# Fewer fp32 steps in the second layer, and an earlier split of four weight rows

## The chip, the cores and the metric

One core of one Trainium2 chip runs the kernel. The metric is the device time of one execution in microseconds, as the median of several runs. TensorE (PE) multiplies matrices, VectorE (DVE), ScalarE (ACT) and GpSimd (POOL) work on tiles in on-chip memory, and SyncE (SP) issues most of the loads and stores. Each engine works through a list of instructions of its own in a fixed order; where an instruction needs another engine's result, it waits, and everything behind it on that engine waits too.

## The reference

The reference is an attention over a small memory, followed by a feed-forward layer with a squared ReLU. There are 8 batches, 8 heads, 576 positions, a head size of 64, 32 memory slots, a model width of 512 and a hidden width of 2048; all in fp32.

```python
a = softmax(phi, axis=seq)                       # (8, 8, 576, 32)
k_m = einsum('bhsm,bhsd->bhmd', a, k)
v_m = einsum('bhsm,bhsd->bhmd', a, v)            # 32 rows of 64 for each head
attn = softmax(q @ k_m^T / 8, axis=-1)           # (8, 8, 576, 32)
x = (attn @ v_m), heads side by side             # (4608, 512)
h = maximum(x @ w_in, 0)                         # (4608, 2048)
out = (h * h) @ w_out                            # (4608, 512)
```

## The kernel before

**The algebra.** x @ w_in is never formed from x. For each batch the kernel multiplies v_m by w_in once, which gives u (32 slots x 8 heads = 256 rows, 2048 columns), and then h = attn @ u. Matmuls in full fp32 are avoided mostly: a number is split into a rounded fp32r part ("hi") and the remainder ("lo"), and a product is taken as hi x hi + lo x hi + hi x lo, three fp32r matmuls for one fp32 matmul.

**The stages.** Batches 0 and 1 go through a fused part of 56 steps (`steps`, at line 878), in which both layers are computed; later batches go through the first layer and, from about 419 us on, through a second layer of another form, neither of which the diff touches. A fused step k takes one block f of 128 hidden units and one group of tokens (b, t): 320 tokens for t = 0, 256 for t = 1. Steps 0 to 3 are f = 0 to 3 of group (0,0), steps 4 to 7 the same rows of (0,1), steps 8 to 11 of (1,0), steps 12 to 15 of (1,1). Step k consists of `ffn1` (h at L696, six matmuls; relu on ScalarE at L704; the square at L708 on ScalarE or at L710 on VectorE), then of half-step 2k of the side work, then of `ffn2` of step k - 2 (`LEAD = 2`; the second layer, sums in the accumulators acc), then of half-step 2k + 1.

**Whole and split rows.** In a step below `WHOLE` with f in 0 to 3, the second layer is done in full fp32: g is one fp32 tile and `ffn2` has four matmuls (L739; the trace has two records for each). In other steps ScalarE writes g_hi with a second square (L720), VectorE or GpSimd writes g_lo (L724; VectorE if k is in `LO_DVE`), and `ffn2` has twelve fp32r matmuls (L747) on a split weight row. `SQ_ACT` names the steps whose square is on ScalarE.

**The weights.** They come as 64-bit words and are decoded (`decode`): ScalarE reads a tile twice (L599, L602), VectorE has three instructions (L604, L607, L612), and VectorE or GpSimd the last (L619). Rows f = 0 to 3 of w_out are decoded whole for the fp32 steps; `split_out` later splits such a row: a copy (L670) and a cast (L676) on ScalarE, a DMA of the whole row that ScalarE issues (L678), and the remainder on VectorE (L679).

**The attention of a group.** Scores on PE (L429), a transpose on VectorE (L460), the maximum (L466), the difference (L472), the exponential on ScalarE (L474), the sum (L477), the reciprocal (L483), the product (L488), the transpose back (L491), then a_hi on ScalarE (L494) and a_lo on GpSimd (L495). h of the group's first step needs both. The scores of group (1,0) need the memory of batch 1 (`task_mem`: L361, L371, L387 to L398, and copies to the tile mem at L406 by VectorE and ScalarE).

**What sets the order.** `loads` is the order in which the first tiles are asked for on SP's queue, of which eight may be under way at a time. The string `order` interleaves, by generator steps, the exponentials, memories, decodes (d0 to d3), attention (a0, a1) and u of batch 0 ahead of step 0. `plan` is a table of side work: each entry names a generator and the half-steps at which its successive pieces are issued. An earlier half-step puts a piece ahead of more work in every engine's list that it uses; it is no time.

Of the kernel before, what the change touches and what calls it, by code (L numbers as in the profile page):

```python
# [24 lines left out]
def attn_moe_kernel(ctx: ExitStack, tc: tile.TileContext, qT, kv, phi, w_in, w_out, outT):  # L25
# [659 lines left out]
    def ffn1(f, parts, T, turn, square, whole):  # L685
# [237 lines left out]
    def next_kv():  # L923
# [30 lines left out]
    later = [x[0] for x in loads].index(task_phi)  # L954
    for fn, *args in loads[:later]:
# [28 lines left out]
    for n in kept:  # L984
# [2 lines left out]


    plan = [
        ((3, 5, 5, 6, 6, 7), task_exp, 1),  # L990
        ((6, 6, 7), decode_out, 2, nc.vector, True),
        ((1,), fetch_w_in, 5, 1),
        ((14, 16, 16), decode_in, 2, 0, nc.gpsimd),
        ((13,), fetch_w_in, 6, 1),
        ((11,), fetch_w_in, 4, 0),
        ((10, 10, 10, 10, 11, 11, 12), task_attend, 1, 0),
        ((11,), fetch_w_in, 5, 0),
# [4 lines left out]
        ((21,), fetch_w_in, 7, 1),
        ((21, 22, 22), decode_in, 3, 1, nc.vector),
        ((26,), fetch_w_in, 7, 0),
        ((25, 29, 29), task_u, 1, 1),
        ((44, 44, 44), decode_in, 5, 1, nc.vector),
        ((45,), fetch_w_out, 10),
        ((31, 32, 33), decode_in, 4, 0, nc.vector),
        ((28,), fetch_w_in, 6, 0),
# [3 lines left out]
        ((25, 30, 30, 32, 32), decode_out, 5, nc.vector),
        ((32, 34, 37), task_u, 0, 1),
        ((33, 34, 35, 37, 40), decode_out, 7, nc.vector),
        ((17, 22, 22), decode_in, 3, 0, nc.vector),
        ((40, 42, 42), decode_in, 4, 1, nc.vector),
        ((50, 51, 54, 54, 54), decode_out, 10, nc.vector),
        ((46, 47, 47, 50, 51), decode_out, 8, nc.gpsimd),
        ((55,), fetch_w_out, 11),  # L1020
        ((54, 55, 55, 56, 59), decode_out, 9, nc.vector),
        ((20, 23, 24, 26, 27), decode_out, 4, nc.vector),
        ((36,), fetch_w_out, 9),
        ((49, 50, 51), task_u, 0, 2),
        ((58,), fetch_w_out, 12),
        ((65, 68, 68), decode_in, 7, 1, nc.vector),
        ((56, 60, 61), task_u, 1, 2),
        ((60, 61, 63), decode_in, 6, 0, nc.vector),
        ((68,), fetch_w_out, 15),
        ((70, 72, 73, 75, 77), decode_out, 12, nc.vector),  # L1030
        ((74,), fetch_w_out, 14),
        ((73, 73, 74), task_u, 0, 3),
        ((63, 65, 65), decode_in, 6, 1, nc.vector),
        ((58, 59, 61, 64, 65), decode_out, 11, nc.vector),
        ((66, 67, 69), decode_in, 7, 0, nc.vector),
        ((57,), task_phi, 2),
        ((76, 77, 77, 79, 79), decode_out, 13, nc.vector),
        ((53,), task_kv, 2, 0),
        ((86,), task_q, 2, 0),
        ((77, 80, 82, 83, 84, 84), task_exp, 2),  # L1040
        ((79,), task_kv, 2, 1),
        ((77, 78, 78, 79, 82), decode_out, 14, nc.vector),
# [10 lines left out]
        ((89, 90, 91, 91, 91, 94, 96), task_attend, 2, 0),
        ((91,), task_stream, 0),
        ((89,), u_slots.give, 5),
        ((89,), task_q, 2, 1),
        ((105,), task_stream, 2),
        ((97,), task_phi, 3),
        ((108,), task_q, 3, 0),
        ((90,), task_kv, 3, 0),  # L1060
        ((96,), task_kv, 3, 1),
        ((98,), task_stream, 1),
        ((101, 102, 103, 104, 105, 106, 107), task_both, 2, 1, 0),
        ((107, 108, 108, 110, 111, 113), task_exp, 3),
        ((107, 108, 109), task_u, 2, 1),
        ((2,), lambda: spin(3, ident)),
        ((2, 4, 4), decode_out, 1, nc.gpsimd, True),
        ((2,), task_q, 1, 1),
        ((2, 2, 3), task_u, 0, 0, HC, 2 * HC),
        ((8, 8, 9, 9), task_mem, 1),  # L1070
        ((5, 7, 9), decode_out, 3, nc.gpsimd, True),
        ((0, 3, 3, 4, 5, 6), lambda: start["a1"]),
# [92 lines left out]
    for k, step in enumerate(steps):  # L1165
# [346 lines left out]
```

## Time and profile before

| | |
|---|---|
| median of 3 runs | 702.66 us (701.67 to 705.85) |
| the profiled execution | 700.55 us |
| its span in the trace | 698.8 us |
| PE, VectorE, ScalarE, GpSimd busy | 98%, 74%, 58%, 9% of the span |
| granted clock of PE | 1.00 in all stages |
| moved by DMA | 133.59 MB, 191 GB/s in the mean |

The span lies 1.75 us below the time of the profiled execution. A busy share near 100% for an engine means that time can be saved only by giving that engine less to do, or by closing its few gaps; but the share is a mean over stages, so the stages are looked at one by one below. An engine's idle time costs something only where another engine waits for it.

### The profile page before, as it was taken

What the parts mean: (1) busy time and instruction counts of PE and PEld (TensorE: products, weight loads), DVE (VectorE), ACT (ScalarE), POOL (GpSimd) and SP (SyncE); (2) the same over time, 40 slices, a digit from 0 to 9 for tenths busy, and PEclk for the clock granted to TensorE, in tenths of its full rate; (3) what the DMA queues carried; (4) which work ended last, traced back from release to release, by engine and by line L of the source; (5) the groups of instructions that cost most, each with busy time, mean ns of one, the idle gap of its engine ahead of it and who ended that gap; (6) DMA issues with size and microseconds to landing.
All of it is one profiled execution on the core that took longest, in us unless ns stands there. A gap on an engine that the chain in (4) does not pass through costs nothing.

```text
span 698.8 us, 14434 instructions
## 1 busy us (share of the span) xinstructions
PE 686.7 (98%) x5860; PEld 613.1 (88%) x5860; DVE 515.2 (74%) x883; ACT 402.8 (58%) x617; POOL 59.7 (9%) x86
## 2 busy tenths in 40 slices
PE   9899999999999999999999999999999999999996
PEld 5477798978888787878787899999999999999996
DVE  4978797887756848484847305889988979697984
ACT  2647887876554454545455555575646464555551
POOL 1322102102221000000000000000000000000000
PEclk9999999999999999999999999999999999999999
DMA  9993527263694969695944468663353534434331
GB/s 309 390 330 127 205 104 236 68 212 118 195 339 169 302 229 301 208 301 191 307 177 171 161 212 298 215 196 103 111 167 105 166 107 136 136 122 151 91 121 61
DMA packets 94355, 133.59 MB, mean 191 GB/s; under 512 B 5520, under 2 KB 59408, under 8 KB 93648
## 3 DMA queue, kind: packets, MB, share of 16 engines
q1 hardware_dynamic: 91472, 127.62, 55.8%
q10 hardware_dynamic: 2816, 5.05, 2.0%
q8 instruction: 46, 0.75, 0.5%
q14 instruction: 21, 0.17, 0.1%
HBM read 86.51 MB, written 46.14 MB: 190 GB/s over the span
## 4 chain that ended last, share of the span: by engine, by line
PE 89%; DMA 5%; DVE 3%; ACT 1%; issue 0%; ACTq 0%; POOL 0%; DVEq 0%
PE b L1300 33%; PE hh L1432 22%; PE acc L747 11%; PE h L696 7%; PE ps_m L429 5%; PE b L1283 4%; PE acc L739 3%; PE h L306 2%; DMA wo<-in_w_out 1%; DMA wo<-in_w_in 1%; PE h L429 1%; DMA wo<-in_kv 1%; DMA kvb<-in_kv 1%; DVE x_lo L1234 1%; PE h L1432 0%
## 5 line engine op out<-in xcount | busy, mean ns | idle before, releaser
L1230 ACT CAST x_hi<-y 128x1792 fp32r<-128x1792 f32 (+1 forms) x56 | 88.0, 1571 | 96.5 <-PE b L1300 52.4
L1234 DVE TENSOR_TENSOR x_lo<-y,x_hi 128x1792 fp32r<-128x1792 f32 (+1 forms) x56 | 104.7, 1870 | 51.8 <-ACT x_hi L1230 49.0
L1463 ACT ACTIVATE o<-hh 128x576 f32<-128x576 f32 x94 | 61.3, 652 | 89.2 <-PE hh L1432 73.5
L1300 PE MATMUL b<-x_lo,s_hi 128*128 128x256 f32 x384 | 108.0, 281 | 0.0
L1300 PE MATMUL b<-x_hi,wo 128*128 128x256 f32 x576 | 107.9, 283 | 0.0
L1300 PE MATMUL b<-x_hi,s_hi 128*128 128x256 f32 x384 | 107.8, 281 | 0.0
L1300 PE MATMUL b<-x_hi,s_lo 128*128 128x256 f32 x384 | 107.8, 281 | 0.0
L1300 PEld LDWEIGHTS b<-x_hi,wo 128*128 128x128 f32 x576 | 89.9, 192 | 0.0
L1300 PE MATMUL b<-x_lo,wo 128*128 128x256 f32 x288 | 81.5, 283 | 0.5 <-DVE x_lo L1234 0.5
L1223 DVE TENSOR_TENSOR y<-y 128x512 f32<-128x512 f32 x144 | 73.7, 512 | 3.3
L1300 PEld LDWEIGHTS b<-x_hi,s_hi 128*128 128x128 f32 x384 | 73.7, 192 | 0.0
L1300 PEld LDWEIGHTS b<-x_lo,s_hi 128*128 128x128 f32 x384 | 72.1, 188 | 0.0
L1300 PEld LDWEIGHTS b<-x_hi,s_lo 128*128 128x128 f32 x384 | 72.1, 188 | 0.0
L1213 ACT ACTIVATE y<-raw 128x1024 f32<-128x1024 f32 (+1 forms) x56 | 57.4, 1025 | 12.1 <-DMA raw<-r_f 8.3
L1300 PEld LDWEIGHTS b<-x_lo,wo 128*128 128x128 f32 x288 | 55.3, 192 | 0.9 <-DVE x_lo L1234 0.9
L578 DVE TENSOR_TENSOR u_lo<-ps_m,u_hi 128x1024 fp32r<-128x1024 f32 (+1 forms) x33 | 38.8, 1176 | 13.3 <-ACT u_hi L576 13.1
L1432 PEld LDWEIGHTS hh<-a_hi,u_hi 128*128 128x128 f32 x188 | 29.4, 188 | 20.5 <-ACT o L1463 15.9
L1432 PE MATMUL hh<-a_hi,u_hi 128*128 128x288 f32 x188 | 43.8, 314 | 0.0
L747 PE MATMUL acc<-g_hi,wo 128*128 128x320 f32 (+1 forms) x256 | 43.2, 301 | 0.0
L1432 PE MATMUL hh<-a_hi,u_lo 128*128 128x288 f32 x188 | 40.2, 295 | 0.0
L1432 PE MATMUL hh<-a_lo,u_hi 128*128 128x288 f32 x188 | 40.1, 294 | 0.0
L704 ACT ACTIVATE r_room<-h 128x320 f32<-128x320 f32 (+2 forms) x56 | 24.7, 442 | 25.6 <-PE h L696 25.3
(240 smaller groups left out, 1435.8 us busy)
## 6 DMA issues: line engine op xcount, KB each, us to landing
r_f<-o SPq DMA_DIRECT2D x48, 576.0 KB, 3.8
raw<-r_f SPq DMA_DIRECT2D x48, 512.0 KB, 4.0
wo<-in_w_in SPq DMA_DIRECT2D x16, 512.0 KB, 8.6
wo<-in_w_out SPq DMA_DIRECT2D x16, 512.0 KB, 7.9
kvb<-in_kv SPq DMA_DIRECT2D x28, 256.0 KB, 5.2
q_sb<-in_q SPq DMA_DIRECT2D x24, 288.0 KB, 4.2
out_t<-m SPq DMA_DIRECT2D x24, 256.0 KB, 2.2
e_sb<-in_phi SPq DMA_DIRECT2D x8, 512.0 KB, 4.7
```

What stands on the lines that cost most here:

```text
L429: nc.tensor.matmul(out[half][M * pr:M * (pr + 1), :y.shape[-1]], mem[hs, x, pr], y, start=True, stop=True)
L578: nc.vector.tensor_tensor(out=u_lo[:, :, n0:n1], in0=ps[:, :, :n1 - n0], in1=u_hi[:, :, n0:n1].bitcast(F32), op=ALU.subtract)
L696: nc.tensor.matmul(h[:, at:at + n], u[:, qd, fs], x[:, qd], start=(i == 0), stop=(i == len(todo) - 1))
L747: nc.tensor.matmul(acc[e][:, :T], wo[f][:, w, e * P:(e + 1) * P], x, start=first and x is g_hi and w == 0, stop=last and x is g_lo,)
L1213: nc.scalar.activation(y[i][:, :2 * n], raw.pop(i), AF.Square)
L1223: nc.vector.tensor_tensor(out=out, in0=in0, in1=in1, op=ALU.subtract)
L1230: nc.scalar.copy(x[i][0], y[i])
L1234: nc.vector.tensor_tensor(out=x[i][1], in0=y.pop(i), in1=x[i][0].bitcast(F32), op=ALU.subtract)
L1283: nc.tensor.matmul(acc[e][:, :n], wo[f][:, v, e * P:(e + 1) * P], x[i][u][:, f % 2 * n:(f % 2 + 1) * n], start=f == 0 and j == 0, stop=f = ...
L1300: nc.tensor.matmul(acc[m][:, e * HALF:(e + 1) * HALF], w, x[i][u][:, z * HALF:(z + 1) * HALF], start=p == 0 and e == 0 and j == 0, stop=p ...
L1432: nc.tensor.matmul(banks[t][:, :T], u[:, qd, fs], x[:, qd], start=(i == 0), stop=(i == len(todo) - 1))
L1463: nc.scalar.activation(r.rearrange("p (t x) -> p t x", t=NT), h[:, :, :S // NT], AF.Relu)
```

## The change

`WHOLE` falls from 16 to 4: steps 4 to 15 take twelve fp32r matmuls in the second layer, not four in fp32, and have a g_hi and a g_lo. For that the rows f = 0 to 3 of w_out are split in half-steps 8 to 16, not 80 to 91. In steps 4 to 15, g_lo is on VectorE in steps 4, 5, 6 and 12 and on GpSimd in the others, and the square moves to VectorE in steps 7 and 13. `loads`, `order` and the places of `plan` are changed too; of `plan`'s some 85 entries the diff shows those that the text speaks of.

```diff
@@ -864,9 +864,9 @@
         yield
 
     LEAD = 2
-    SQ_ACT = (0, 1, 2, 3, 4, 5, 6, 7, 8, 9, 10, 11, 12, 13, 14, 15, 16, 17, 18, 19, 20, 21, 23, 24, 25, 26, 27, 28, 29, 30, 31, 32, 33, 34, 35, 36, 37, 39, 40, 42, 43, 44, 45, 47, 48, 50, 52, 53, 54, 55, 56, 58,)
-    LO_DVE = (-1, 16, 17, 18, 19, 20, 21, 22, 23, 27, 28, 32, 33, 34, 35, 36, 37, 39, 40, 41, 48, 49, 52, 56, 57, 58, 59, 60, 61, 62, 63, 64,)
-    WHOLE = 16
+    SQ_ACT = (0, 1, 2, 3, 4, 5, 6, 8, 9, 10, 11, 12, 14, 15, 17, 18, 20, 21, 22, 23, 25, 26, 27, 28, 29, 31, 32, 33, 34, 36, 37, 39, 40, 41, 44, 45, 46, 49, 50, 53, 54, 55, 56, 59, 60, 61,)
+    LO_DVE = (-1, 0, 1, 4, 5, 6, 12, 19, 20, 22, 23, 24, 26, 31, 36, 38, 40, 42, 43, 45, 47, 48, 49, 50, 52, 54, 56, 57, 58, 59, 62, 63, 64,)
+    WHOLE = 4
     Q4 = NFT // 4
 
 
@@ -927,29 +927,29 @@
     loads = [
         (first_phi,),
         (first_kv, 0),
+        (fetch_w_in, 0, 1),
         (first_kv, 1),
         (fetch_w_in, 0, 0),
+        (task_q, 0, 1),
         (task_q, 0, 0),
-        (task_q, 0, 1),
-        (fetch_w_in, 0, 1),
         (fetch_w_in, 1, 0),
+        (fetch_w_out, 4),
+        (fetch_w_out, 0),
         (fetch_w_in, 1, 1),
-        (fetch_w_in, 2, 0),
         (fetch_w_out, 3),
         (task_phi, 1),
+        (fetch_w_out, 5),
+        (fetch_w_out, 1),
+        (fetch_w_in, 2, 0),
+        (task_kv, 1, 0),
+        (fetch_w_out, 2),
         (fetch_w_out, 6),
-        (fetch_w_out, 0),
-        (fetch_w_out, 1),
-        (fetch_w_out, 2),
         (fetch_w_in, 3, 0),
+        (fetch_w_in, 2, 1),
         (task_q, 1, 0),
-        (fetch_w_out, 4),
+        (next_kv,),
         (fetch_w_out, 7),
-        (task_kv, 1, 0),
-        (next_kv,),
         (fetch_w_in, 3, 1),
-        (fetch_w_out, 5),
-        (fetch_w_in, 2, 1),
     ]
     later = [x[0] for x in loads].index(task_phi)
     for fn, *args in loads[:later]:
@@ -972,7 +972,7 @@
     }
 
     order = (
-        "e e e e e m d0 m m d0 d0 m d0 a0 d1 d0 d2 a1 a0 a0 a0 a0 a0 a0 d1 d1 d1 d1 d3 a0 a0 a0 a0 a0 a0 a0 a0 u0 d3 u0 d3 d3 a0 d3 u0 a0 d2 d2 d2 d2"
+        "e e e e e d1 d0 m m m d0 d1 m d1 d2 a0 d0 d0 a0 a1 a0 a0 a0 a0 a0 d1 d0 a0 a0 a0 a0 d1 d2 a0 a0 u0 d2 a0 d3 d3 a0 u0 d3 a0 u0 d2 d2 d3 d3 a0"
     )
     for x in order.split():
         if callable(start[x]):
@@ -987,91 +987,91 @@
     plan = [
...
-        ((80, 82), split_out, 0),
-        ((87, 87), split_out, 1),
-        ((89, 91), split_out, 2),
-        ((83, 83), split_out, 3),
+        ((8, 9), split_out, 0),
+        ((8, 11), split_out, 1),
+        ((9, 9), split_out, 2),
+        ((14, 16), split_out, 3),
...
-        ((24, 28, 28, 30, 31), decode_out, 6, nc.gpsimd),
+        ((31, 31, 31, 35, 35), decode_out, 6, nc.gpsimd),
-        ((17, 18, 19), decode_in, 2, 1, nc.gpsimd),
+        ((12, 12, 15), decode_in, 2, 1, nc.gpsimd),
...
```

The first place is on PE, at the copies of batch 1's memory: the transposes that the memory is made with (L398), then h of step 5 and the scores of group (1,0). Before:

```order
L398 MATMUL ps_m<-ident,st 128x128 x4
L696 MATMUL h<-a_hi_506,u_hi_334 128x256 x2
L696 MATMUL h<-a_hi_506,u_lo_335 128x256 x2
L696 MATMUL h<-a_lo_507,u_hi_334 128x256 x2
L429 MATMUL ps_m<-q_sb,mem 32x320 x8
L739 MATMUL acc_496<-g_hi,wo_623 128x320
```

and now:

```order
L398 MATMUL ps_m<-ident,st 128x128 x4
L429 MATMUL ps_m<-q_sb,mem 32x320 x8
L696 MATMUL h<-a_hi_517,u_hi_331 128x256 x2
L696 MATMUL h<-a_hi_517,u_lo_332 128x256 x2
L696 MATMUL h<-a_lo_518,u_hi_331 128x256 x2
L739 MATMUL acc_491<-g_hi,wo_557 128x320
```

The scores (q_sb by mem, 320 tokens) stood behind the three passes of h; now they are ahead of them.

The second place is on VectorE, from the copy to mem to the sum of the softmax of group (1,0). Before:

```order
L406 COPY mem<-ps_m 64x256
L460 STREAM_TRANSPOSE st<-ps_m 128x320 x2
L466 TENSOR_REDUCE mx<-st 128x20
L472 TENSOR_TENSOR st<-st,mx 128x640
L477 TENSOR_REDUCE sm<-st 128x20
```

and now, from the g_lo of step 4 on (wo_583, wo_652 and wo_579 are the split rows 0, 2 and 1 in the order of issue):

```order
L724 TENSOR_TENSOR g_lo<-g_room,g_hi 128x256
L679 TENSOR_TENSOR wo_583<-tmp,wo_583 128x512
L406 COPY mem<-ps_m 64x256
L679 TENSOR_TENSOR wo_652<-tmp,wo_652 128x512
L460 STREAM_TRANSPOSE st<-ps_m 128x320 x2
L466 TENSOR_REDUCE mx<-st 128x20
L472 TENSOR_TENSOR st<-st,mx 128x640
L724 TENSOR_TENSOR g_lo<-g_room,g_hi 128x256
L679 TENSOR_TENSOR wo_579<-tmp,wo_579 128x512
L477 TENSOR_REDUCE sm<-st 128x20
```

Two g_lo and three remainders of split rows (L679) have come in; two of the remainders stand on either side of the copy to mem.

The third place is on ScalarE, between the exponential of the same softmax (L474, one to four rows above) and its a_hi. Before, from the last copy of an accumulator:

```order
L784 COPY o_661<-acc_499 128x320
L576 CAST u_hi_679<-ps_m 128x1024
L704 ACTIVATE r_room<-h 128x256
L708 ACTIVATE g_hi<-r_room 128x256
L494 CAST a_hi_677<-at 128x640
```

and now:

```order
L784 COPY o_688<-acc_494 128x320
L678 DMA w_out_f_0_88<-tmp 128x512
L576 CAST u_hi_705<-ps_m 128x1024
L704 ACTIVATE r_room<-h 128x256
L708 ACTIVATE g_room<-r_room 128x256
L720 ACTIVATE g_hi<-r_room 128x256
L599 ACTIVATE tmp<-wo_390 128x512
L602 ACTIVATE low<-wo_390 128x512
L494 CAST a_hi_703<-at 128x640
```

A DMA issue, a g_hi and the two reads of a weight tile (wo_390, a part of w_in) have come in ahead of L494.

The fourth place is on PE again, the second layer of step 4 with the last pass of h of step 6 ahead of it. Before:

```order
L696 MATMUL h<-a_lo_507,u_hi_334 128x256 x2
L739 MATMUL acc_704<-g_hi,wo_434 128x256
L739 MATMUL acc_705<-g_hi,wo_434 128x256
L739 MATMUL acc_706<-g_hi,wo_434 128x256
L739 MATMUL acc_707<-g_hi,wo_434 128x256
```

and now:

```order
L696 MATMUL h<-a_lo_518,u_hi_331 128x256 x2
L747 MATMUL acc_737<-g_hi,wo_583 128x256 x2
L747 MATMUL acc_738<-g_hi,wo_583 128x256 x2
L747 MATMUL acc_739<-g_hi,wo_583 128x256 x2
L747 MATMUL acc_740<-g_hi,wo_583 128x256 x2
L747 MATMUL acc_737<-g_lo,wo_583 128x256
L747 MATMUL acc_738<-g_lo,wo_583 128x256
L747 MATMUL acc_739<-g_lo,wo_583 128x256
L747 MATMUL acc_740<-g_lo,wo_583 128x256
```

Four matmuls have become twelve.

## Rows read from the trace of the kernel before

**Rows 1.** The page, part 4: shares of the chain that ended last.
```profile
PE 89%; DMA 5%; DVE 3%; ACT 1%; issue 0%; ACTq 0%; POOL 0%; DVEq 0%
```

**Rows 2.** Windows: stretch, length, PE, PEld, DVE, ACT, POOL busy, PEclk, DMA share, GB/s.
```profile
0.00:43.10 43.10, 38.29 (x253) 22.02 (x254) 31.78 (x76) 20.80 (x41) 11.69 (x23) 1.00 1.01 340
43.10:62.30 19.20, 18.90 (x207) 14.16 (x205) 13.10 (x26) 9.79 (x22) 2.83 (x2) 1.00 0.67 243
62.30:91.60 29.30, 29.30 (x182) 23.42 (x175) 24.20 (x44) 24.32 (x52) 5.63 (x4) 1.00 0.41 153
91.60:136.80 45.20, 45.20 (x352) 43.14 (x351) 37.80 (x70) 37.81 (x85) 7.07 (x8) 1.00 0.46 151
136.80:212.90 76.10, 76.10 (x587) 64.61 (x586) 55.83 (x118) 47.36 (x92) 16.30 (x23) 1.00 0.67 217
```

**Rows 3.** Chain of waits, 60 to 140 us: start, length, what.
```profile
61.76 0.59 PE ps_m L429 x16
...
67.75 2.15 PE acc L739 x8
...
83.04 1.73 PE acc L739 x8
...
93.65 1.36 PE acc L747 x12
...
100.39 1.76 PE acc L747 x12
```

**Rows 4.** Chain of waits, 0 to 62 us (ACTq is ScalarE issuing a DMA).
```profile
1.96 0.49 ACTq L915
...
50.43 0.43 DVE mem L406
...
50.88 0.38 ACT mem L406
...
51.30 0.85 PE ps_m L429 x16
...
58.79 0.73 ACT a_hi L494
...
59.59 1.56 POOL a_lo L495
...
61.19 0.56 PE h L696 x2
```

**Rows 5.** ScalarE's timeline, 48 to 62 us: start, length, instruction, [idle before, releaser].
```profile
54.84 0.74 ACT L474 ACTIVATE st<-st 128x640 f32<-128x640 f32 x1 [2.73 <-DVE st L472]
...
58.79 0.72 ACT L494 CAST a_hi<-at 128x640 fp32r<-128x640 f32 x1 [0.27 <-DVE at L491]
...
60.15 0.66 ACT L599 ACTIVATE tmp<-wo 128x512 f32<-128x512 f32 x1
```

**Rows 6.** VectorE's timeline, 50 to 62 us.
```profile
52.17 0.92 DVE L460 STREAM_TRANSPOSE st<-ps_m 128x320 f32<-128x320 f32 x2 [1.33 <-PE ps_m L429]
...
55.60 0.82 DVE L477 TENSOR_REDUCE sm<-st 128x20 f32<-128x640 f32 x1 [0.80 <-ACT st L474]
```

**Rows 7.** Groups by line and shape: count, busy us, mean ns, idle before.
```profile
L724 POOL TENSOR_TENSOR g_lo<-g_room,g_hi 128x320 fp32r<-128x320 f32 x12 | 10.8, 907 | 36.0 <-ACT g_hi L720 14.9 <-PE h L696 6.4 <-PE acc L747 5.9
L679 DVE TENSOR_TENSOR wo<-tmp,wo 128x512 fp32r<-128x512 f32 x16 | 10.8, 684 | 5.3 <-ACT wo L676 5.3
...
L676 ACT CAST wo<-tmp 128x512 fp32r<-128x512 f32 x16 | 9.8, 614 | 5.6 <-DVE tmp L619 4.1 <-POOL tmp L619 1.3
...
L720 ACT ACTIVATE g_hi<-r_room 128x256 fp32r<-128x256 f32 x8 | 3.2, 401 | 0.0
```

**Rows 8.** GpSimd's timeline, 66 to 76 us.
```profile
70.45 1.76 POOL L495 TENSOR_TENSOR a_lo<-at,a_hi 128x512 fp32r<-128x512 f32 x1 [2.73 <-ACT a_hi L494]
```

**Rows 9.** VectorE's timeline: the same sum beside that instruction and alone.
```profile
71.22 1.54 DVE L619 CUSTOM_DVE_ANT_0 w<-tmp,low 128x1024 uint16<-128x1024 uint16 x1
...
44.94 0.69 DVE L619 CUSTOM_DVE_ANT_0 wo<-tmp,low 128x1024 uint16<-128x1024 uint16 x1
```

More of the change, by code (lines that the diff above doesn't have):

```diff
@@ L989, in attn_moe_kernel @@
     plan = [
[L990 to L997, printed above, removed]
-        ((11, 11, 11), task_u, 1, 0),
-        ((14,), fetch_w_in, 4, 1),
-        ((16, 16, 18, 18, 19, 20, 21), task_attend, 1, 1),
@@ L1001, in attn_moe_kernel @@
-        ((17, 18, 19), decode_in, 2, 1, nc.gpsimd),
[L1002 to L1009, printed above, removed]
-        ((24, 28, 28, 30, 31), decode_out, 6, nc.gpsimd),
-        ((37,), fetch_w_out, 8),
-        ((36, 37, 38), decode_in, 5, 0, nc.vector),
@@ L1013, in attn_moe_kernel @@
[L1013 to L1042, printed above, removed]
-        ((83, 83), split_out, 3),
-        ((75, 75, 76), task_u, 1, 3),
-        ((75,), fetch_w_out, 13),
-        ((80, 82), split_out, 0),
-        ((78, 80, 80, 82, 82), decode_out, 15, nc.gpsimd),
@@ L1048, in attn_moe_kernel @@
-        ((87, 87, 87, 88, 88), task_mem, 2),
-        ((87, 90), ahead, 0),
-        ((87, 87), split_out, 1),
-        ((112,), task_stream, 3),
-        ((89, 91), split_out, 2),
[L1053 to L1072, printed above, removed]
@@ L1073, in attn_moe_kernel @@
-        ((0, 0, 1), decode_out, 0, nc.gpsimd, True),
-        ((6,), lambda: spin(1, ident)),
+        ((27, 27, 27), task_u, 1, 1),
+        ((5,), fetch_w_in, 6, 1),
+        ((85,), task_stream, 3),
+        ((52, 52, 55), task_u, 0, 2),
+        ((22, 22, 22, 29, 30), decode_out, 4, nc.vector),
+        ((109, 110, 110), task_u, 2, 1),
+        ((87, 87, 87, 87, 88), task_mem, 2),
+        ((67,), task_kv, 2, 0),
+        ((3,), lambda: spin(3, ident)),
+        ((94,), task_kv, 3, 1),
+        ((69, 69, 70), decode_in, 7, 0, nc.vector),
@@ new lines, in attn_moe_kernel @@
+        ((9, 9), split_out, 2),
+        ((3, 5, 5, 6, 6, 6), task_exp, 1),
+        ((101,), task_kv, 3, 0),
+        ((7, 7, 7), decode_out, 2, nc.vector, True),
+        ((104,), task_phi, 3),
+        ((8, 11), split_out, 1),
+        ((34, 37, 37), decode_in, 4, 0, nc.vector),
+        ((94,), task_stream, 0),
+        ((78, 82, 82, 86, 87), decode_out, 15, nc.gpsimd),
+        ((14, 16), split_out, 3),
+        ((87, 94), ahead, 0),
+        ((35, 37, 37), task_u, 0, 1),
+        ((65,), fetch_w_out, 14),
@@ new lines, in attn_moe_kernel @@
+        ((63,), fetch_w_out, 13),
+        ((88,), task_q, 2, 1),
+        ((8, 9), split_out, 0),
+        ((105,), task_q, 3, 0),
+        ((25, 30, 30, 32, 32), decode_out, 5, nc.vector),
+        ((0, 0, 2), decode_out, 0, nc.gpsimd, True),
+        ((59, 62, 67), task_u, 1, 2),
+        ((47, 49, 51, 52, 52), decode_out, 8, nc.gpsimd),
+        ((24,), fetch_w_out, 8),
+        ((53, 60, 60), decode_in, 6, 0, nc.vector),
+        ((25,), fetch_w_in, 6, 0),
+        ((2, 2, 3), task_u, 0, 0, HC, 2 * HC),
@@ new lines, in attn_moe_kernel @@
+        ((0, 3, 4, 5, 5, 5), lambda: start["a1"]),
+        ((50, 51, 52, 54, 54), decode_out, 10, nc.vector),
+        ((88, 90, 91, 91, 97, 99, 102), task_attend, 2, 0),
+        ((52,), fetch_w_out, 11),
+        ((106, 106, 109, 109, 113, 113), task_exp, 3),
+        ((77, 78, 78, 78, 78), decode_out, 13, nc.vector),
+        ((65, 65, 69), decode_in, 7, 1, nc.vector),
+        ((6,), lambda: spin(1, ident)),
+        ((2, 3, 4), decode_out, 1, nc.gpsimd, True),
+        ((63, 64, 68), decode_in, 6, 1, nc.vector),
@@ new lines, in attn_moe_kernel @@
+        ((15, 15, 18, 18, 20, 20, 20), task_attend, 1, 1),
+        ((31, 31, 31, 35, 35), decode_out, 6, nc.gpsimd),
+        ((21, 21, 21), decode_in, 3, 1, nc.vector),
+        ((2,), fetch_w_in, 4, 0),
+        ((96,), task_stream, 2),
+        ((34,), fetch_w_out, 9),
+        ((79, 79, 82, 82, 84, 85), task_exp, 2),
+        ((7,), fetch_w_in, 4, 1),
+        ((38, 40, 44), decode_in, 5, 0, nc.vector),
+        ((86,), task_q, 2, 0),
+        ((5, 7, 7), decode_out, 3, nc.gpsimd, True),
+        ((16, 20, 20), decode_in, 3, 0, nc.vector),
@@ new lines, in attn_moe_kernel @@
+        ((89,), u_slots.give, 5),
+        ((44, 44, 44), decode_in, 5, 1, nc.vector),
+        ((72,), task_phi, 2),
+        ((18,), fetch_w_in, 5, 0),
+        ((65,), fetch_w_out, 15),
+        ((40, 43, 47), decode_in, 4, 1, nc.vector),
+        ((69, 71, 74, 76, 76), decode_out, 12, nc.vector),
+        ((12, 12, 15), decode_in, 2, 1, nc.gpsimd),
+        ((76, 76, 76), task_u, 1, 3),
+        ((77, 78, 83, 83, 83), decode_out, 14, nc.vector),
+        ((59,), fetch_w_out, 12),
+        ((46,), fetch_w_in, 7, 0),
@@ new lines, in attn_moe_kernel @@
+        ((8, 8, 9, 9), task_mem, 1),
+        ((73, 73, 73), task_u, 0, 3),
+        ((43,), fetch_w_out, 10),
+        ((8,), fetch_w_in, 5, 1),
+        ((32, 32, 32, 39, 40), decode_out, 7, nc.vector),
+        ((0,), task_q, 1, 1),
+        ((55, 58, 59, 59, 62), decode_out, 9, nc.vector),
+        ((9, 10, 10, 10, 11, 11, 13), task_attend, 1, 0),
+        ((80,), task_kv, 2, 1),
+        ((60, 61, 62, 63, 65), decode_out, 11, nc.vector),
+        ((14, 16, 19), decode_in, 2, 0, nc.gpsimd),
@@ L1075, in attn_moe_kernel @@
+        ((96,), task_stream, 1),
+        ((25,), fetch_w_in, 7, 1),
+        ((101, 101, 103, 104, 104, 104, 104), task_both, 2, 1, 0),
+        ((11, 11, 11), task_u, 1, 0),
     ]
```

## The prediction

> **What bounds the kernel now.** I read the page's chain first, then the windows by stage, then the chain of waits in order of time where the change acts, and last the single instructions. TensorE carries 89% of the chain; DMA has 5%, VectorE 3% [rows 1]. So a change is worth what it does to PE's work, plus or minus the few gaps in which PE waits. The windows say where such gaps are [rows 2]: up to 43.1 us PE is busy 38.29 and the DMA share is 1.01, at 340 GB/s, so the start goes at the rate of the loads; in 43.1 to 62.3 PE lacks 0.3 us; in 62.3 to 91.6 it is busy for all 29.30, and from there to 212.9 us it never stops. VectorE and ScalarE have room in these stretches (24.20 and 24.32 of 29.3). The granted clock is 1.00 throughout, the upper level of 2.4 GHz.
>
> Steps 4 to 15 of the fused part, which the change rewrites, have their second-layer products between about 56 and 91.6 us. That is where the time must be won or lost.
>
> **Part 1: 12 fp32r matmuls for 4 fp32 ones (each a pair of records in the trace), in steps 4 to 15.** The chain prices both forms, for 320 and for 256 tokens [rows 3]: 2.15 against 1.76 us, and 1.73 against 1.36. A step therefore gives back 0.39 (320 tokens: steps 8 to 11) or 0.37 (256 tokens: steps 4 to 7 and 12 to 15). The products of steps 6 to 15 lie where PE has no idle time: 4 x 0.39 + 6 x 0.37 = **-3.8 us**. Those of steps 4 and 5 stand ahead of a wait, so their 0.74 goes into part 2. The Trainium skill ("FP8 and Floating Point Precision", TensorE Precision Notes) says that true fp32 takes four passes through the array. Three fp32r products would then take three quarters of the time, 1.61 for 2.15, and the ten steps would give 4.8 by that estimate; the rows show 1.76, so the sum stays with them.
>
> **Part 2: the first wait, at step 8.** Step 8 is the first of a new group of tokens, (1,0). Its h needs a_hi and a_lo at the end of that group's softmax. Before, ScalarE writes a_hi at 58.79, GpSimd makes a_lo from 59.59 to 61.15, and PE uses it at 61.19 [rows 4]. The change puts work ahead of this on both engines.
>
> - VectorE's order now has the remainder of the split of row 2 (L679, 0.68 [rows 7]) between the copy of mem and the transpose of the scores (L460). That L679 waits for ScalarE: mem's copy at 50.88, 0.38 long [rows 4], then the split's copy and cast, 0.61 each [rows 7] (the row is the cast's, the copy has the same shape), which ends at 52.5; with L679 it is 53.1 before L460 can start, where it started at 52.17 [rows 6]. So the softmax starts 0.95 later. Ahead of the sum (L477) stand two more, L724 of step 5 (0.4, taken as the square of the same size [rows 7]) and the L679 of row 1, together 1.1, of which the 0.80 that L477 waited [rows 6] takes most: VectorE is then 1.25 late.
> - ScalarE, between the exp (L474) and a_hi (L494), had 0.27 idle [rows 5]. It gets one g_hi (L720, 0.40 [rows 7]), the two reads of a weight tile that is decoded (L599 as shown, 0.66 [rows 5], and L602 of the same shape), and the issue of a DMA on its queue (L678; the nearest row is 0.49, at the start [rows 4], I take 0.33): 2.05, less the 0.27 and some overlap of neighbours, 1.7 late on top of the 0.95. That is later than VectorE. So a_lo is ready 2.6 later, at 63.75.
> - PE comes there with 0.74 less work from steps 4 and 5. But the scores (L429) now stand ahead of h of step 5, so the 0.85 us of mem's two copies (50.43 to 51.30 [rows 4]), which h filled, stay empty; and 0.59 of the second scores [rows 3] were moved ahead of step 8. It arrives no later than 61.19 - 0.74 + 0.85 + 0.59 = 61.9 and waits 1.85 or more. Before, the same work, second scores included, was done at 61.19 + 0.59 = 61.78; now a_lo comes at 63.75.
>
> I take **+2.0 us**, inclusive of the gain of steps 4 and 5. Bounds: +0 where ScalarE finds the decode's reads and the squares early enough to do them while it waits for L474 or L491, so that only VectorE's 1.25 arrives and the 0.59 of the second scores and the 0.74 cover it; +3.5 where the weight tile whose reads stand ahead of a_hi lands late by one load, 1.5 us (part 4).
>
> **Part 3: g_hi and g_lo of steps 4 to 15, the splits.** Every fp32r step needs one more square on ScalarE and a subtraction. In 62.3 to 91.6 us ScalarE gets eight g_hi (0.40 each for 256 tokens [rows 7], a little more for 320: 3.4) and the split of row 3 (1.2); it loses one square to VectorE (0.4) and the reads of one tile that is decoded later (1.3). That is 24.32 + 2.9 = 27.2 of work for a stretch of 29.3 - 3.8 = 25.5 us: 1.7 too much. PE runs two steps behind the squares, and after 91.6 ScalarE has 7 us of room (37.81 of 45.2 [rows 2]), so most of the excess is carried past. I take **+0.5**, with bounds 0 and +1.7. The eight g_lo on GpSimd, 0.91 each [rows 7], fit in GpSimd's time, 5.63 of 29.3 now; what they may do to VectorE is a rival below. The splits that leave half-steps 80 to 91 give nothing: they lie in 136.8 to 212.9, where PE is busy for 76.10 of 76.1 [rows 2].
>
> **Part 4: the order of loads, the first part.** The same bytes go through the same queue. w_in(0,1) is moved ahead of the second half of kv, and 1 MB of loads ahead of q(0,0); w_in(1,0), whose decode stands ahead of the first exp on ScalarE in both orders, has the same bytes ahead of it. The last piece of batch 1's kv comes one tile later, 1.5 us (524 KB at 340 GB/s [rows 2]). I take **0**, since the exp's tile sets the first h, with bounds -1 (w_in(0,1) is read sooner) and +3 (two tiles). Later loads, planned for other half-steps, are cut off from PE by the full stretches of [rows 2]: 0.
>
> **Sum.** 0 + 2.0 - 3.8 + 0.5 = -1.3 us. The profiled execution took 700.55 us (698.8 of span and 1.75 around it); the sum makes it 699.25. The median of the three runs is 702.66, 2.1 above the profiled one, and I carry this difference along: **701.4 us**.
>
> **Rivals.**
>
> *A, the full gain.* The wait at step 8 stays where it was and the excess on ScalarE is carried past: all twelve steps count, -(3.8 + 0.74) = -4.5, and 698.1 us. For it: 0.27 and 2.73 us of ScalarE's idle time stand just there [rows 5]. Against it: four more instructions stand in one row between exp and a_hi.
>
> *B, slower: VectorE held up by GpSimd.* One meeting shows it [rows 8, 9]: a L619 on VectorE takes 1.54 us while GpSimd's L495 runs, which itself takes 1.76; alone, L619 takes 0.69. With those eight g_lo on GpSimd where VectorE now works 24.2 of 25.5 us, at 0.85 lost for each, VectorE would have 6.8 more and end 5.5 behind: +2.0 - 3.8 + 5.5 = +3.7, 706.4 us. It decides from the third such meeting on, when VectorE has no room left. The Trainium skill ("SBUF — State Buffer", Who interferes with whom) has the rule behind it: a VectorE instruction with two SBUF inputs contends with a GpSimd instruction that reads SBUF. The row agrees for that pair. Against it: most of VectorE's work here has one input from PSUM or a constant beside the tile.
>
> *C, a later start.* The moved loads put the first group's softmax two tiles later and nothing after gives it back: +3 - 1.3 = +1.7, 704.4 us. The loads are at their limit up to 43 us, so an order counts; but the tile that stands at the first exp keeps its place.
>
> *D, the change does nothing:* products for the steps still go whole. The order of PE has twelve matmuls from step 4 on, so this is left with 1%: 702.7.
>
> **Chances.** Forecast (its own range 699.5 to 703) 0.45, A 0.24, B 0.16, C 0.14, D 0.01. The range leaves out a tenth at either side: below A by part 4's gain of 1, 697.1; above it takes in B, 706.5. One per cent, 7 us, is about what a measurement here can tell from no change. Faster than 695.6 needs all of A and 2.6 us that no row shows: 0.05. Slower than 709.7 needs B and C together, with part 2 at its upper bound: 0.05. Within: 0.90.
>
> **What would show it.** Chain entries of the second layer in steps 4 to 15 at 1.36 and 1.76 us show part 1 right. A wait of PE on GpSimd's L495 of about 2 us near 62 us shows part 2; if there is none, A holds. PE idle on ScalarE's squares between 65 and 91 us beyond 0.5 would show part 3 mis-sized; L724 rows on GpSimd beside VectorE instructions of double length, with PE waiting, would show B. The copy of mem later than 50.9 us by more than 1 shows C. I am wrong altogether if the time changes after 91.6 us.

## The result and the profile after

The changed kernel takes 708.97 us in the median (708.75 to 711.95, 5 runs) against 702.66 us for the kernel before (701.06 to 705.85, 5 runs): a ratio of 1.0103, with a 95% interval of 1.0074 to 1.0133 (the medians alone give 1.0090). It is 6.3 us slower, and 7.6 us above the forecast of 701.4. The profiled execution has a span of 707.2 us, 8.4 more than before.

The page's busy times and its chain, which answer to [rows 1]:

```profile
PE 686.7 (97%) x5908; PEld 616.3 (87%) x5908; DVE 531.1 (75%) x892; ACT 403.3 (57%) x621; POOL 70.9 (10%) x97
...
PE 75%; DVE 10%; DMA 7%; ACT 5%; issue 2%; SPq 1%; DVEq 0%; ACTq 0%
```

PE is as busy in sum as before, 686.7 us, but its share of the chain fell from 89% to 75%; VectorE's rose from 3% to 10% and ScalarE's from 1% to 5%. The windows by stage, with the columns of [rows 2]:

```profile
0.00:43.10 43.10, 37.83 (x250) 21.23 (x251) 32.01 (x73) 18.35 (x37) 10.39 (x23) 1.00 1.00 339
43.10:62.30 19.20, 17.05 (x190) 13.05 (x188) 15.34 (x30) 13.32 (x29) 2.55 (x2) 1.00 0.65 233
62.30:91.60 29.30, 25.56 (x198) 23.14 (x197) 26.24 (x39) 24.45 (x56) 13.03 (x12) 0.94 0.34 126
91.60:136.80 45.20, 43.26 (x339) 40.02 (x338) 40.01 (x68) 35.35 (x76) 11.02 (x11) 0.96 0.43 149
136.80:212.90 76.10, 75.80 (x588) 66.74 (x587) 60.86 (x119) 43.91 (x86) 14.94 (x21) 1.00 0.67 213
```

Where PE had no idle time before, it now lacks 3.7 us in 62.3 to 91.6 and 1.9 in 91.6 to 136.8, and the granted clock is below 1. The chain of waits there (start, length, what) shows who holds it:

```profile
62.58 0.47 DVE u_lo L578
63.06 0.34 DVE tmp L604
63.42 0.44 DVE tmp L607
63.89 2.01 DVE tmp L612
...
67.89 1.37 DVE wo L679
69.27 1.03 DVE tmp L604
70.32 0.44 DVE tmp L607
70.78 0.69 DVE tmp L612
71.48 1.28 DVE st L472
72.78 0.63 ACT st L474
73.72 2.77 PE acc L747 x12
76.50 1.60 PE h L696 x6
78.10 1.83 PE acc L747 x12
79.93 0.71 PE h L696 x6
80.63 1.76 PE acc L747 x12
```

Before, this stretch was PE from end to end. Now VectorE's list runs almost without a gap until the softmax of group (1,1) reaches ScalarE's exponential (L474). Behind that exponential on ScalarE stand the copies of the accumulators of step 7 (L784). There is one set of four accumulators, so the second layer of step 8 cannot begin before. PE's waits between 45 and 112 us (engine and line, whom it waited for, total, times, longest):

```profile
PE acc L747 <- ACT o L784: 2.0, 1, 2.0
PE h L696 <- DVE g_room L710: 1.9, 1, 1.9
PE acc L739 <- DVE wo L619: 1.2, 1, 1.2
PE acc L747 <- DVE wo L679: 1.0, 1, 1.0
PE ps_m L429 <- ACT mem L406: 0.9, 1, 0.9
PE h L696 <- POOL a_lo L495: 0.8, 1, 0.8
```

After each of the two long ones the granted clock falls; the windows of 5 us (columns as above) give 0.69 and 0.66, where both levels, 1.2 and 2.4 GHz, are mixed:

```profile
75.00:80.00 5.00, 5.00 (x27) 5.00 (x26) 4.69 (x7) 4.36 (x9) 2.58 (x3) 0.69 0.00 0
105.00:110.00 5.00, 5.00 (x27) 4.89 (x26) 4.65 (x9) 3.40 (x10) 1.16 (x1) 0.66 0.68 270
```

### The profile page after: what moved, and what is told of

It reads as the page before. It is cut to its first block, busy times and chain, and to the rows that moved or that the text cites. A ratio compares the mean times of both kernels' runs of the same rounds, so it can differ in the third digit from the quotient of the medians.

```text
span 707.2 us, 14564 instructions
## 1 busy us (share of the span) xinstructions
PE 686.7 (97%) x5908; PEld 616.3 (87%) x5908; DVE 531.1 (75%) x892; ACT 403.3 (57%) x621; POOL 70.9 (10%) x97
## 4 chain that ended last, share of the span: by engine, by line
PE 75%; DVE 10%; DMA 7%; ACT 5%; issue 2%; SPq 1%; DVEq 0%; ACTq 0%
PE b L1300 34%; PE hh L1432 20%; PE acc L747 6%; PE b L1283 5%; PE ps_m L429 4%; PE h L696 3%; DMA wo<-in_w_in 3%; PE h L306 2%; DMA w<-w_f 2%; DMA e_sb<-in_phi 2%; DVE tmp L612 1%; PE h L429 1%; DVE tmp L604 1%; DMA raw<-r_f 1%; DVE tmp L607 1%
## 5 line engine op out<-in xcount | busy, mean ns | idle before, releaser
L747 PE MATMUL acc<-g_hi,wo 128*128 128x320 f32 (+1 forms) x352 | 60.2, 303 | 3.0 <-ACT o L784 2.0
L747 PEld LDWEIGHTS acc<-g_hi,wo 128*128 128x128 f32 x352 | 52.5, 191 | 4.6 <-ACT o L784 2.2
```

What stands on the lines that cost most here:

```text
L747: nc.tensor.matmul(acc[e][:, :T], wo[f][:, w, e * P:(e + 1) * P], x, start=first and x is g_hi and w == 0, stop=last and x is g_lo,)
```

## The experiments

The table follows PE: by how much the first matmul of h starts later than before in step 5, step 12, step 23 and at the last h of the fused part, read from PE's timeline of one profiled execution each, then the span. The last column is the ratio of times to the kernel before on the same chip. The trace of the kernel before is of an execution 2.1 us below its median (e2's is 2.5 below its own), so most spans look up to 2 us worse than the ratios, which decide.

| run | step 5 | step 12 | step 23 | last h | span | ratio (95%) |
|---|---|---|---|---|---|---|
| the change | +4.0 | +7.2 | +8.7 | +7.2 | +8.4 | 1.0103 (1.0074 to 1.0133) |
| e1 core, g_lo on GpSimd | -0.2 | +3.4 | +5.0 | +3.2 | +4.4 | 1.0049 (1.0031 to 1.0066) |
| e2 core, g_lo on VectorE | -0.3 | +1.1 | +2.9 | +1.2 | +1.1 | 1.0036 (1.0019 to 1.0054) |
| e3 order alone | +3.4 | +1.9 | +1.9 | +3.6 | +6.5 | 1.0078 (1.0060 to 1.0097) |
| e16 early part of the order | +4.0 | +2.5 | +2.5 | +2.6 | +4.0 | 1.0027 (1.0014 to 1.0040) |
| e17 middle of the plan | +0.2 | +0.2 | +0.3 | +0.6 | +1.6 | 1.0012 (0.9998 to 1.0027) |
| e18 core and middle | +0.1 | +3.6 | +5.7 | +4.3 | +5.9 | 1.0060 (1.0031 to 1.0088) |
| e13 PE shorter | -0.2 | -1.4 | -0.7 | -0.6 | +1.0 | 0.9993 (0.9983 to 1.0003) |
| e14 more load | +0.9 | +1.2 | +3.4 | +3.5 | +3.5 | 1.0040 (1.0027 to 1.0052) |

**The core alone: e1 and e2.** The kernel before with

```diff
-    WHOLE = 16
+    WHOLE = 4
-        ((80, 82), split_out, 0),
+        ((8, 9), split_out, 0),
-        ((87, 87), split_out, 1),
+        ((8, 11), split_out, 1),
-        ((89, 91), split_out, 2),
+        ((9, 9), split_out, 2),
-        ((83, 83), split_out, 3),
+        ((14, 16), split_out, 3),
```

and, in e2, steps 4 to 15 added to `LO_DVE`.

> The core of the change alone on the kernel before: fp32 in the first 4 steps only, the four splits early, nothing else; all twelve new g_lo are on GpSimd. Theory 1 (GpSimd's g_lo hold up VectorE): PE waits on VectorE between 62 and 110 us, 706 to 710 us. Theory 2 (the retimed order and loads of the change are to blame): the core alone gains, 698 to 701 us, memory of batch 1 copied at 50.4 as before. Theory 3 (ScalarE is overfull): 704 to 706 us with PE waiting on ScalarE's squares.

> As the first, with the twelve new g_lo on VectorE (12 x 0.45 = 5.4 us more for it, no meeting with GpSimd's g_lo). Theory 1: at least 4 us better than with GpSimd, 699 to 704 us. Theory 2: like the first, 698 to 702 us. Theory 3: like the first, 704 to 706 us.

e1 took 704.95 us and e2 704.23, against 702.26. The core, which should gain, loses 2.7 and 2.0 us. On which engine the g_lo are matters little, so theory 1 falls for the core. Theory 3 gave both numbers (e2's just) but not the wait: PE waits most on the copies of the accumulators (L784, 4.1 us in e1 and 2.7 in e2), not on ScalarE's squares. Behind step 23 both regain 1.7 to 1.8 us; this is the hidden wait at 177 us that e9 and e15 below are about.

**The order alone, and all g_lo on VectorE: e3 and e4.** e3 is the change with `WHOLE = 16` and the splits in their old half-steps; e4 is the change with steps 7 to 11 and 13 to 15 added to `LO_DVE`.

> The change without its core: the new loads, order, plan and the two engine tables, but fp32 in the first 16 steps and the splits late as before. Theory 1: without the g_lo of steps 4 to 15 the time is that of before or up to 3 us more for the later start, 702 to 706 us. Theory 2: the stalls stay and the gain of the products is gone, 710 to 714 us. Theory 3: 702 to 705 us.

> The change with all g_lo of steps 4 to 15 on VectorE (8 more there, 3.5 us of work). Theory 1: the stretched VectorE instructions between 62 and 92 us (5.7 us now) go, 703 to 706 us. Theory 2: within 1.5 us of the change, 708 to 710 us. Theory 3: 708 to 711 us, since VectorE gets work and ScalarE loses none.

e3: 707.89 us, 5.6 more than before, with the work of before in another order and, by the engine tables, in part on another engine; that lies between theories 1 and 3 (to 706 and 705) and theory 2 (from 710). e4: 709.88, no better than the change. VectorE is stretched beside GpSimd in the change, as rows of VectorE and GpSimd show (start, length, instruction):

```profile
63.89 2.01 DVE L612 SCALAR_TENSOR_TENSOR tmp<-wo,tmp 128x512 int32<-128x512 int32 x1
```

```profile
63.80 1.55 POOL L495 TENSOR_TENSOR a_lo<-at,a_hi 128x640 fp32r<-128x640 f32 x1 [15.55 <-ACT a_hi L494]
```

L612 takes 0.69 elsewhere (at 70.78 in the chain above). The rule that the prediction cited from the Trainium skill ("SBUF — State Buffer", Who interferes with whom) agrees with this pair. L679 at 67.89 and L604 at 69.27 in the chain are long as well (1.37 and 1.03, against 0.68 in [rows 7] and 0.34 at 63.06), with GpSimd's L619 and L724 beside them. e4 is no clean test of what this costs: it takes the g_lo off GpSimd, but L612 still takes 2.01 us beside L495, and VectorE, which now has eight more g_lo, delivers one of them so late that PE waits 3.3 us, which the change does not have:

```profile
63.23 2.01 DVE L612 SCALAR_TENSOR_TENSOR tmp<-wo,tmp 128x512 int32<-128x512 int32 x1
```

```profile
PE acc L747 <- DVE g_lo L724: 3.3, 1, 3.3
```

So a g_lo on VectorE costs no less than one on GpSimd; the price of the meetings in the change is not shown.

**Single stalls taken away: e5 to e8.** e5 (on the change) and e8 (on e2) issue the exponential of group (1,1) a half-step later, behind the copies; e6 puts two matmuls of the identity into the stall; e7 has the loads and the first part's string of before.

```diff
-        ((15, 15, 18, 18, 20, 20, 20), task_attend, 1, 1),
+        ((15, 15, 19, 19, 20, 20, 20), task_attend, 1, 1),
```

```diff
+        ((20,), lambda: spin(2, ident)),
```

The first is e5's (in e8 the entry is 16, 16, 18, 18, 19, 20, 21 and its two 18 become 19), the second e6's.

> The change with the exponential of group (1,1) (L474) issued one half-step later, so that ScalarE copies out the accumulators of step 7 (L784) ahead of it. Theory 4 (PE waits at the change of groups since the copies of the single accumulators stand behind that late exponential, and the stall makes the clock fall): the wait of 2.0 us on L784 and the stretch at half the clock behind it go, about 3.5 us, 704.5 to 706.5 us. Theory 3 (ScalarE is simply overfull): the wait moves to the next squares, 708 to 709.5 us.

> The change with two matmuls of the identity (1.0 us in the trace of before, four records) put into PE's list just ahead of the second layer of step 8, in the stall of 2.0 us on L784; the work is otherwise the same. Theory 4a (the fall of the granted clock after the stall costs 1.6 us by itself): the clock stays at 1.00 in 75 to 80 us, 706.5 to 708 us. Theory 4b (the fall costs nothing, since PE would wait behind it anyway): the time of the change, 708.5 to 710 us.

> The change with loads and the order of the first part (the list and the string) as before; the plan and the core as in the change. Theory 2 (the new start costs 3.4 us at step 5 of which 1.9 stay): 704.5 to 707.5 us. If the later excess of work hides the start: 708 to 709.5 us.

> The core alone on the kernel before with all new g_lo on VectorE, and the exponential of group (1,1) one half-step later, behind the copies of the accumulators. Theory 4: the wait of 1.3 us on L784 at step 8 goes, 701 to 703 us. Theory 3: ScalarE, busy without a gap from 55.6 to 72.7 us there, moves the wait to another place, 703.5 to 705 us.

None gained clear of the noise: 709.93, 709.39 and 709.93 us against 708.97 for the change, and 705.60 against 704.23 for e2 (before: 703.20 on this chip, 702.66 and 702.26 on theirs). The ratios of e5, e6 and e7 are 1.0106 (1.0070 to 1.0142), 1.0088 (1.0063 to 1.0112) and 1.0097 (1.0072 to 1.0122) against 1.0103, and e8's is 1.0040 (1.0023 to 1.0057) against 1.0036. By their times, e5, e7 and e8 lie a little above what any theory gave (to 709.5, 709.5 and 705). In e5 the wait on L784 is gone and PE is at +4.1 in step 12 where the change has +7.2, but it then waits 2.2 us on VectorE's L710 at 103 us and is at +7.6 in step 23. In e6 the clock stays up:

```profile
62.30:91.60 29.30, 27.27 (x212) 23.73 (x212) 26.50 (x40) 24.10 (x56) 12.74 (x12) 1.00 0.34 126
91.60:136.80 45.20, 42.75 (x339) 39.09 (x339) 40.36 (x70) 36.14 (x78) 11.02 (x11) 1.00 0.45 152
```

PE is then at +6.4 in step 23, 2.3 better than the change, and as much at the last h (+4.9), but the span of this execution is +8.2. So theory 4 names a real stall, and taking it away gives none of the 3.5 us that it forecast. The 1.6 us of theory 4a are not seen, and e6's interval does not exclude them. e7 still has +3.5 in step 5, and e18 below, with the core but the plan's first entries of before, +0.1: the later start is not due to the loads, as rival C had it, but to the plan's first entries.

**Splits and load: e9 to e11.** e9 and e15 (below) are the kernel before with two splits moved; e10 is the kernel before with `WHOLE = 8`, splits in half-steps 15 to 24, g_lo of steps 8 to 15 on VectorE; e11 is e1 with

```diff
+        plain = not whole and turn < 16
...
+        if plain:
+            return (g, g), []
```

where g is an fp32r tile, so that L720 and L724 are left out of steps 4 to 15.

> The kernel before with only the splits of rows 1 and 2 taken from half-steps 87 and 89 to 84 and 85, ahead of the copies of batch 2's memory (L338). Theory 5 (the scores at 177.17 us in the trace of before, 16 matmuls in 2.54 us against 0.77 elsewhere, hide a wait of 1.77 us on a VectorE that stands behind a split's remainder, so that the early splits of the change gain 1.77): 1.3 to 2.0 us less than before on the same chip. My prediction's view (PE is busy there, the splits cost nothing): within 0.5 us of before.

> The kernel before with fp32 in the first 8 steps, the splits in half-steps 15 to 24, and the 8 new g_lo on VectorE. Theory 3 (the extra work of ScalarE and VectorE in 55 to 75 us, around the change of groups at step 8, costs more than the products give): with that stretch spared, 8 steps give 3.0 and the splits' absence from 80 to 91 another 1.8, 2 to 4 us less than before. Theory 6 (any split ahead of step 16 and any g_lo there stalls PE as much as it gives): between 1 us less and 2 us more.

> The core alone on the kernel before, but in steps 4 to 15 the square is written once in fp32r and used for all twelve matmuls: g_hi (L720) and g_lo (L724) of these steps are left out, the matmuls and the early splits stay (the low part of the square is not computed). Theory 3: without the 12 squares on ScalarE and the 12 subtractions all of the gain is seen, 5 to 6.5 us less than before. Theory 7 (the early splits at half-steps 8 to 16 make the stalls): 0 to 2 us less than before.

e9: 702.65 us against 702.56. The hidden wait at 177 us went, but a wait of 2.1 us on GpSimd's L724 (for h at L306) came just ahead of it. e10: 712.44, and the reason is a new one, on ScalarE:

```profile
86.89 0.66 ACT L599 ACTIVATE tmp<-wo 128x512 f32<-128x512 f32 x1 [5.17 <-DMA w_out_f<-tmp]
```

A split's store (L678) landed late, held one of the three buffers named tmp, and the next decode waited 5.17 us for it, with the accumulators' copies behind. e11: 704.97, with a smaller wait of the same kind (2.9 us). So neither theory 3 nor 6 is tested by e10, and e11's 704.97, which no theory gave, is no measure of the g work; up to step 18 it was only 0.2 us behind the kernel before, where e1 was 4.0.

**PE and the others one at a time: e13 and e14.**

```diff
+            n = T - 64 if f and short[0] else T
-                    acc[e][:, :T], wo[f][:, e * P:(e + 1) * P], g_hi, start=first, stop=last
+                    acc[e][:, :n], wo[f][:, e * P:(e + 1) * P], g_hi[:, :n], start=first, stop=last
```

```diff
+        if whole and turn >= 4:
+            nc.scalar.activation(g, r, AF.Square)
+            return (g, None), [lambda: nc.vector.tensor_tensor(out=g, in0=r, in1=r, op=ALU.mult)]
```

The first is e13's, in `ffn2` (short is set from step 4 on), the second e14's, in `ffn1`.

> The kernel before, in which only PE gets less to do: the fp32 products of steps 5 to 7, 9 to 11 and 13 to 15 take 64 tokens fewer (these parts of the second layer are left out); 0.42 us less a step by the two chain lengths of 320 and 256 tokens, 2.6 to 3.8 us in all. Theory 10 (what PE gains ahead of 92 us is lost at once, since it only arrives earlier at work that VectorE and ScalarE deliver just in time): at most 1.2 us less than before. Theory 3 (the new work on the other engines is what costs): the gain is seen, 2.2 to 3.8 us less than before.

> The kernel before, in which only ScalarE and VectorE get more to do: in steps 4 to 15 the square is made a second time on ScalarE and once more on VectorE, in the places of g_hi and g_lo, with no change on PE, fp32 and late splits as before. Theory 3: PE waits at the changes of groups as in the core alone, 3 to 6 us more than before. Theory 10: PE is as late as before, so that most is hidden, at most 2 us more.

These two decide. e13 took 701.56 us against 702.16: of the 2.6 to 3.8 us that PE was to be spared, 0.6 came out, within the uncertainty. Its waits between 56 and 105 us, where the kernel before has none:

```profile
PE acc L748 <- DVE wo L679: 1.0, 1, 1.0
PE h L696 <- POOL a_lo L495: 0.5, 1, 0.5
PE ps_m L429 <- DVE w L619: 0.2, 1, 0.2
```

PE was 1.9 us ahead at 95 us by its timeline, and the first of these (with the slow pass behind it) took 1.2 back at once. e14 took 705.08 us, 2.9 more (1.9 to 3.7 by the interval), with PE's work as before: the extra squares and products alone. Of its +3.5 at the last h, 0.9 was there before step 4, in a start with a granted clock of 0.96, and is not the load's. Its waits between 45 and 105 us:

```profile
PE acc L742 <- ACT o L787: 0.5, 1, 0.5
PE ps_m L429 <- ACT mem L406: 0.2, 1, 0.2
PE h L696 <- POOL a_lo L495: 0.2, 1, 0.2
PE h L696 <- DVE u_lo L578: 0.2, 1, 0.2
```

Only the first is like the core's, at the copies of the accumulators (L784 in the other kernels), and it is far smaller than the 4.1 and 2.7 us there. Another 0.8 us is lost between steps 12 and 13, where the sixteen matmuls that make u take 1.9 us instead of 1.1 and no wait is listed. Theory 10 holds for the gain. The cost lies above theory 10's 2 and just below theory 3's 3 to 6: load on ScalarE and VectorE costs time with nothing added on PE, but where PE loses it is shown only in part.

**The order in parts: e12, e15 to e18.** e12 has the plan's entries from half-step 20 on and the two engine tables, e16 the loads, the string and the entries ahead of 20, e17 the entries from 20 to 83 and the tables; e18 is the change with start and end of before. e15 is the kernel before with

```diff
-        ((87, 87), split_out, 1),
-        ((89, 91), split_out, 2),
+        ((92, 92), split_out, 1),
+        ((94, 94), split_out, 2),
```

(and e9 with 84, 84 and 85, 85).

> Of the change only the entries of the plan that begin in half-step 20 or later, with its two engine tables; loads, the first part, the plan up to half-step 20, fp32 steps and splits as before. Theory 8 (the early entries cost 1.9 us that stay, the late ones the rest of the 5.6 us that the whole order costs): 3 to 4.5 us more than before. Theory 9 (all of the order's loss starts at steps 1 to 5): within 1 us of before.

> The kernel before with only the splits of rows 1 and 2 in half-steps 92 and 94, behind the copies of batch 2's memory (L338) and its softmax, where neither VectorE's transposes nor ScalarE's g_hi of the broad steps stand behind them. Theory 5: the hidden wait of 1.77 us at 177 us goes and nothing takes its place, 1.3 to 2.0 us less than before. Otherwise: a new wait of the same length, within 0.6 us of before.

> Of the change only the loads, the order of the first part and the entries of the plan that begin ahead of half-step 20; late entries, engine tables, fp32 steps and splits as before. Theory 8: h of step 5 is 3.4 us late as in the whole order, of which 1.5 to 2.5 us stay at the end. Theory 9 (the early part alone makes the loss): 5 to 6 us more than before.

> Of the change only the plan's entries that begin in half-steps 20 to 83, with its two engine tables; everything else as before. Theory 11 (the late loss comes from the streams, u and loads of batches 2 and 3 that the change places at half-steps 85 to 113, seen as waits of PE at 212 to 236 us): at most 1.5 us more than before, no wait of PE on a streamed weight there. Otherwise (the middle of the plan loses): 3 to 4.5 us more, as with the late entries too.

> The change with everything but its core, its engine tables and the middle of its plan (half-steps 20 to 83) as before: the loads, the first part, the plan up to half-step 20 and from 84 on are those of before. By the sum of the parts (early 1.6, late about 2 to 3 of the change's 6.3): 2 to 3.5 us more than before, as the core alone. If the losses of start and end are hidden behind the core's own: 5 to 6.5 us more.

e12: 706.72 us against 702.56, 4.2 more. e17, the same without the entries from 84 on: 702.70 against 702.58. So the late entries cost some 4 us; a wait at 205 to 240 us that e17 does not have shows 2.2 of it, and the granted clock falls behind it (0.98 in 212.9 to 300):

```profile
PE ps_m L429 <- DVE u_lo L578: 2.2, 1, 2.2
```

In the change's own trace this wait is 1.1 us. e16: 703.78 against 702.16, 1.6 more, with the waits on VectorE's L192 (1.3), L619 (1.2) and mem (0.9) of the change in steps 1 to 5. e18: 706.50 against 702.58, 3.9 more, between its two forecasts (2 to 3.5 and 5 to 6.5). e15: 704.44, 2.3 more where 1.8 less was expected. The row behind theory 5, of the kernel before, and the same scores in e15:

```profile
177.17 2.54 PE L429 MATMUL ps_m<-q_sb,mem 64*32 64x288 f32 x16
```

```profile
177.49 0.78 PE L429 MATMUL ps_m<-q_sb,mem 64*32 64x288 f32 x16
```

PE's waits in e15 from 150 to 230 us:

```profile
PE ps_m L429 <- DMA u_hi<-w_f: 1.9, 1, 1.9
PE acc L747 <- DVE o L774: 0.8, 1, 0.8
PE acc L747 <- POOL tmp L127: 0.4, 1, 0.4
```

In the kernel before the matmuls come one by one at first, spread over the wait. This wait of 1.76 us is real and goes, since VectorE's remainder of a split no longer stands ahead of L338. But the moved work meets other due times: PE loses 5.6 us again up to the last h, 3.1 of it in the waits listed, one of them on a DMA.

## Why the prediction was wrong

- **Part 1 (-3.8 us)** had its prices right: the chain shows 1.76 us for 320 tokens at full clock, as in [rows 3]. Its failing step was "the products of steps 6 to 15 lie where PE has no idle time", taken to mean that PE sets the pace there. e13 shows that it does not alone: spared some 3 us, PE gives 0.6, since decoded weights, remainders and a_lo come just in time, although VectorE is busy for only 24.20 of 29.30 us there [rows 2]. (The estimate beside it, by four passes, adds up to 4.7 and not 4.8; nothing hangs on it.)
- **Part 2 (+2.0 at a_lo)** was right in kind and wrong in place and size. a_lo was ready at 65.35 (63.80 and 1.55 above), 4.2 later than before where 2.6 was forecast, but PE waited only 0.8 on it, since it came to step 8 itself 3.6 late (h at 63.77 against 60.16) by the waits of the start. The longer wait was at the next softmax's exponential, with the copies of the only accumulators behind it: 2.0 us, and the clock's fall after it. Even that one does not set the time by itself (e5).
- **Part 3 (+0.5, "carried past")** was mis-sized: e14 gives +2.9 for such load alone (with all twelve products on VectorE, where the change has eight of its g_lo on GpSimd). The lead of two steps didn't carry it: at each change of groups the copies of the only accumulators come due, and PE's waits of the core alone are there (4.1 us on L784 in e1, 2.7 in e2). That early splits "give nothing" was wrong as well: a merged row of 2.54 us for 16 matmuls that take 0.78 counts as busy and hid 1.76.
- **Part 4 (0)**: the start cost 1.6 (e16), inside the bounds but not by the loads; "Later loads ... are cut off from PE ...: 0" failed, with some 4 us for the entries from half-step 84 on (e12 against e17). "I am wrong altogether if the time changes after 91.6 us" has come true: h of step 18 starts 4.8 us later than before (95.35 against 90.51), that of step 23 8.7.
- **The rivals.** A did not occur. B's sign is there: VectorE's instructions of double length beside GpSimd's, VectorE in the chain, PE waiting. But the core loses 2.0 us with none of the new g_lo on GpSimd (e2), so B is not needed for that part; its share in the rest stays open. C's late start is there (mem is copied at 52.57, before at 50.43) with another cause.
- **The sum.** The core alone costs 2.0 to 2.7, the early part 1.6, the late 4; together more than the 6.3 measured. e18 shows that start and end cost only 2.4 on top of the core and the middle, so a part of one delay hides another; the shorter wait on u_lo in the change (1.1 for 2.2) fits this. How much of e18's 3.9 is the core's and how much its meeting with the middle of the plan stays open.

No version here beats the kernel before; e17 and e9 equal it.

## What to carry to other kernels

An engine that is busy 100% of a stretch need not be the only one that sets its pace: where other engines at 80% deliver each piece just in time, ask what each piece's slack is before a saving on the first is counted. Test it cheaply by leaving out some of that engine's work (e13), and test the price of added work alone (e14). A merged row that is longer than the same instructions elsewhere hides a wait or a lower clock, and moving what causes a wait needs a place where nothing else is due.

## What was not expected of the hardware

The granted clock fell to its lower level for some 3 us after PE had waited 1.96 us, and again after 1.94: the twelve matmuls for 320 tokens took 2.77 us at 73.72 and 1.76 at 80.63 in the chain above. In e6 a wait of 2.2 us on L710 was followed by no fall (1.00 in 91.6 to 136.8), in e5 one of the same length by a fall (0.66 in 103 to 108), so the length of the wait alone does not decide; what does stays open. VectorE's L604 (a tensor_scalar with one input from on-chip memory, which the prediction had taken for safe) took 1.10 us at 69.19, with GpSimd's L724 running from 68.68 to 70.00, against 0.41 at 62.98 in the same trace:

```profile
62.98 0.41 DVE L604 TENSOR_SCALAR tmp<-tmp 128x512 f32<-128x512 f32 x1
...
69.19 1.10 DVE L604 TENSOR_SCALAR tmp<-tmp 128x512 f32<-128x512 f32 x1
```

```profile
68.68 1.32 POOL L724 TENSOR_TENSOR g_lo<-g_room,g_hi 128x320 fp32r<-128x320 f32 x1
```

The Trainium skill ("SBUF — State Buffer", Who interferes with whom) counts tensor_scalar among the operations that can take GpSimd's ports as well; the trace agrees.
